# Four PSUM banks for lone up-projections, scores of the next block beside the value product of the last, and a deeper pipeline for the first token blocks

## The chip, the cores and the metric

One core of a Trainium2 chip runs the whole program. The metric is the device time of one launch in microseconds (us), lower is better. TensorE (PE in the profile, with its weight loads as PEld), VectorE (DVE), ScalarE (ACT), GpSimd (POOL) and SyncE (SP, which here only issues DMAs) each work through an instruction list of their own, in the order in which the program was written, and wait for one another through semaphores.

## The reference

Sliding-window causal attention over 8 sequences of 576 tokens with 8 heads of 64, followed by a two-layer network with a quick-GELU on each of the 4608 tokens. The weights are called `moe_`, but there is one expert and no routing.

```python
scores = (1 / sqrt(64)) * matmul(q, k.transpose(0, 1, 3, 2))     # q, k, v: (8, 8, 576, 64)
mask   = (rel >= 0) & (rel < 64)                                  # rel = query position - key position
attn   = softmax(where(mask, scores, -1e9))
x      = matmul(attn, v), heads side by side                      # (4608, 512)
h      = x @ w_in                                                 # (512, 2048)
out    = (h * sigmoid(1.702 * h)) @ w_out                         # (4608, 512), float32
```

## The kernel before

**Tiles.** The 4608 tokens are 36 *blocks* of 128 tokens (number m) and 9 *chunks* of 512 tokens (number ch, four blocks each). A sequence b has 4.5 blocks of its own, so its rows come in five pieces i of 128 tokens, the fifth of 64. A query reaches 64 keys back, so 64 queries need 128 keys.

**Attention for a block.** `cast_qk` turns a piece of q and k to bf16 (`rows_q`, `rows_k`), `cast_v` that of v. The rows are transposed to `qkt`, either by TensorE (`turn_pe`: eight transposes into the PSUM tile `turn`, then one copy by DVE for q, and after it one by ACT for k) or by a transposing DMA (`turn_dma`). `scores(m)` is 16 small matmuls into the PSUM tile `S`; `exp(m)` on ACT gives `E`; `mask(m)` on DVE multiplies with the band and gives `PT`; `pv(m)` is 16 matmuls into `Tacc`, whose spare column holds the row sum; `norm(m)` on DVE is a reciprocal `rc` and a multiplication to `xs`. `xs` is transposed to `xT`, by TensorE (`x_mm` into `pxt`, then the ACT copy `x_out`) or by DMA (`x_dma`).

**The network.** `up(ch, f, nf, t0, nt)` computes a 128x512 piece of h in one PSUM bank (`hps`): 16 matmuls of 128 columns, 8 of 256 or 4 of 512. ACT takes the tanh (`th`, L284), DVE makes `gT` = (tanh + 1) * h (L287). `down(ch, i)` is four matmuls of 512 columns, and every fourth `down` finishes 128 tokens, which `down_out` copies on ACT (`o_sb`) and sends out, with the DMA issued from ACT's queue (L309).

**PSUM.** Eight banks: `psS` 2 (one `S`), `psT` 2 (one `Tacc` or `pxt`), `psH` 2 (two `hps`, or a `turn`), `psO` 2 (two `ops`, or a `turn` or `pxt`).

**Stages.** The order is written out by hand (`manual_schedule`):
1. *First blocks*: m = 0 to 2, with attention alone, since no `xT` is there yet. `warm(n)` puts n matmuls on nothing into TensorE's list.
2. *Lone ups of chunk 0*: 16 `up`, with `pv(3)` between them.
3. *Downs of chunk 0*: 16 `down`, with the transposes of pieces (0,4) and (1,0) and the attention of block 4 between them.
4. *Lone ups of chunk 1*: four rounds (m = 4 to 7) of four `up`, each with the attention of block m+1 and the arrival of a piece.
5. *Slots 32 to 143*: in each slot one `up` of chunk ch, then one `down` of chunk ch-1. The tables `pe` and `post` hang the rest on slots: a function in `pe[s]` comes between the slot's `up` and `down`, one in `post[s]` at the start of the slot. `scores(m)` stand at `slot_s[m]`, and `mask(m)` and `pv(m)` at `slot_s[m] + 2`, `mask` in `post`, `pv` in `pe`. From block 12 on (chunk 3) `xs` goes to `xT` by DMA.
6. *Last downs*: 16 `down` of chunk 8.

From sequence 3 on the pieces are loaded by `load_bf16` from POOL's queue, transposed by `turn_dma`, and `shift_v` on POOL makes the second copy of v.

Of the kernel before, what the change touches and what calls it, by code (L numbers as in the profile page):

```python
# [9 lines left out]
H = 8  # L10
# [18 lines left out]
def kernel(  # L29
# [17 lines left out]
    th_pool = ctx.enter_context(tc.tile_pool(name="th", bufs=2))  # L47
# [221 lines left out]
    H_of, O_of = {}, {}  # L269

    def up(ch, f, nf, t0, nt):

        ps = psH.tile([P, nf, nt], fp32, name="hps", tag="H")
        for g in range(nf):
            for c in range(4):
# [6 lines left out]
                )  # L282
        th = th_pool.tile([P, nf, nt], bf16, name="th", tag="th")
        nc.scalar.activation(out=th[:], in_=ps[:], func=AF.Tanh, scale=0.851)  # L284
        if (ch, f // 4) not in gT:
# [4 lines left out]
        )  # L290

# [14 lines left out]
    def down_out(ch, tsub):  # L306
        o_sb = ob_pool.tile([P, DM], fp32, name="o_sb", tag="o_sb")
        nc.scalar.activation(out=o_sb[:], in_=O_of.pop((ch, tsub))[:], func=AF.Copy, scale=0.5)  # L308
        nc.scalar.dma_start(out=out_tiled[:, ch * 4 + tsub, :], in_=o_sb[:])  # L309
# [7 lines left out]
    DA = (nc.vector, nc.scalar)  # L317

# [9 lines left out]
    for m in range(3):  # L328
        arrive(0, m + 1)
        if m == 1:  # L330
            for j in range(4):
                load_w_in(j)
        mask(m)
        pv(m)
        norm(m)
        turn_pe(psO, "O", 0, m + 1)
        x_mm(m, psO, "O")
        x_out(m)
        scores(m + 1)
        exp(m + 1)  # L340
        if m < 2:
            warm(4)
# [15 lines left out]
    up(0, 4, 4, P, P)  # L358
    up(0, 4, 4, 2 * P, P)
    up(0, 0, 4, 3 * P, P)  # L360
    up(0, 4, 4, 3 * P, P)
    for f in range(8, 16):
        up(0, f, 1, 0, 512)


    for i in range(16):
        if i % 4 == 0 and i > 0:
            down_out(0, i // 4 - 1)
        if i == 10:
# [4 lines left out]
        if i == 11:  # L374
            scores(4)
            exp(4)
        if i == 13:
# [3 lines left out]
            arrive(1, 1)  # L381
        down(0, i)
    x_mm(4, psH, "H")
    x_out(4)
    turn_pe(psH, "H", 1, 1)
# [3 lines left out]
    b2 = iter([lambda i=i: load_f32(2, i) for i in range(5)])  # L389
    next(b2)()  # L390
    for m in range(4, 8):
        scores(m + 1)
        exp(m + 1)
        t0 = (m % 4) * P
        up(1, 0, 4, t0, P)
        up(1, 4, 4, t0, P)
        mask(m + 1)
        pv(m + 1)
        norm(m + 1)
        if m < 7:  # L400
            arrive(1, m - 2)
        next(b2)()
        if m >= 6:
            cast_qk(2, m - 6, (nc.gpsimd, nc.gpsimd))
# [27 lines left out]
    for m in range(9, NM):  # L432
        if m < 12:
            at(slot_pv[m] + 1, lambda m=m: x_mm(m, psT, "T"), [lambda m=m: x_out(m)])
    for m in range(9, NM):
        at(slot_s[m], lambda m=m: scores(m), [lambda m=m: exp(m)])
        later(slot_pv[m], lambda m=m: mask(m))
        at(slot_pv[m], lambda m=m: pv(m), [lambda m=m: norm(m)])
        if m >= 12:
            later(slot_pv[m] + 1, lambda m=m: x_dma(m))  # L440

    for i in range(2, 5):
        at(32 + 2 * (i - 2), lambda i=i: cast_qk(2, i, (nc.gpsimd, nc.gpsimd)))
        at(32 + 2 * (i - 2), lambda i=i: turn_dma(2, i))
        at(32 + 2 * (i - 2), lambda i=i: cast_v(2, i))
# [64 lines left out]
```

## Time and profile before

| what | value |
|---|---|
| time, median of 3 runs | 351.66 us (350.82 to 353.08) |
| the profiled execution: its own time, its span | 355.03 us, 353.3 us |
| TensorE busy | 310.0 us (88%) |
| VectorE, ScalarE, GpSimd busy | 163.4 us (46%), 158.0 us (45%), 133.5 us (38%) |
| mean granted TensorE clock | 0.985 of full |
| HBM traffic | 36.70 MB read, 9.44 MB written |

Times within the execution are counted from the start of the span. A row of a timeline has start, duration, engine, line, operation, `out<-in`, shapes and a count, and in brackets the idle time of the engine before it with what ended that. A row of the waits says which engine and line stood idle, for whom, for how long in all, how often, and the longest. A matmul's duration includes its way through the pipeline, so that consecutive matmuls overlap in the rows; what TensorE's time is spent on is read from start to start.

### The profile page before, as it was taken

The numbers are of one execution on the slowest core, as the hardware profiler recorded it, in microseconds if no ns is written. First come the engines' busy times: TensorE is split into PE (matmuls) and PEld (weight loads), VectorE is DVE, ScalarE is ACT, GpSimd is POOL, SyncE is SP. The second block draws the span as 40 slices with busy tenths as digits, with TensorE's granted clock in tenths as the row PEclk, the third lists the DMA queues.
The fourth block names the chain that finished last, engine by engine and source line by source line (L and its number), as shares of the span: only waits on it lengthen the run. The fifth ranks groups of instructions, "written<-read, shape, count | busy, mean of one in ns | idle before, by whom it ended". The sixth has DMA issues, their size and how long they took to land.

```text
span 353.3 us, 7859 instructions
## 1 busy us (share of the span) xinstructions
PE 310.0 (88%) x3240; PEld 187.1 (53%) x3240; DVE 163.4 (46%) x285; ACT 158.0 (45%) x249; POOL 133.5 (38%) x190
## 2 busy tenths in 40 slices
PE   2777897677789996999999999999999999999995
PEld 1447343466666664676665665665444444444442
DVE  4535531456554453545445545544545544533400
ACT  3463424555444443444454454444445444444421
POOL 3670043745398589234983923492000000000000
PEclk9998999998899999999999999999999999999999
DMA  9999899946499999799999999993343331110021
GB/s 171 187 182 204 153 202 243 237 95 121 84 121 139 148 158 135 80 132 168 148 117 163 185 148 143 126 113 77 87 94 87 79 76 45 46 59 31 32 75 73
DMA packets 164579, 43.83 MB, mean 124 GB/s; under 512 B 155840, under 2 KB 159936, under 8 KB 164544
## 3 DMA queue, kind: packets, MB, share of 16 engines
q0 software_dynamic: 74544, 13.05, 53.5%
q1 hardware_dynamic: 84816, 20.85, 36.0%
q10 hardware_dynamic: 5184, 9.44, 7.4%
q8 instruction: 25, 0.41, 0.5%
q14 instruction: 10, 0.08, 0.1%
HBM read 36.70 MB, written 9.44 MB: 131 GB/s over the span
## 4 chain that ended last, share of the span: by engine, by line
PE 60%; DVE 17%; ACT 12%; DMA 6%; issue 2%; ACTq 1%; SPq 0%
PE ops L298 26%; PE hps L276 26%; DVE gT L287 8%; ACT th L284 7%; DVE PT L209 6%; PE Tacc L223 4%; DMA xT_dma<-xs 4%; PE S L194 3%; DMA stage<-in_k_dram 3%; ACT E L204 2%; DVE xs L236 2%; ACT o_sb L308 1%; ACT qkt L177 1%; PE turn L171 1%; DVE qkt L177 1%
## 5 line engine op out<-in xcount | busy, mean ns | idle before, releaser
L287 DVE SCALAR_TENSOR_TENSOR gT<-th,hps 128x512 bf16<-128x512 bf16 x144 | 98.9, 687 | 142.4 <-ACT th L284 142.0
L284 ACT ACTIVATE th<-hps 128x512 bf16<-128x512 f32 x144 | 85.9, 597 | 143.2 <-PE hps L276 131.1
L298 PE MATMUL ops<-w_out_sb,gT 128*128 128x512 bf16 x576 | 143.8, 380 | 0.0
L276 PEld LDWEIGHTS <-w_in_sb 128*128 128x128 bf16 x1376 | 102.9, 100 | 51.9 <-issue 6.0
L276 PE MATMUL hps<-xT_dma,w_in_sb 128*128 128x128 bf16 (+2 forms) x704 | 99.4, 282 | 3.1 <-DMA xT_dma<-xs 3.1
L298 PEld LDWEIGHTS <-gT 128*128 128x128 bf16 x576 | 51.2, 98 | 51.5
L276 PE MATMUL hps<-xT_pe,w_in_sb 128*128 128x128 bf16 (+1 forms) x672 | 52.9, 235 | 2.4 <-DVE gT L287 2.1
L102 POOL DMA_DIRECT2D v_nat<-in_v_dram x25 | 21.5, 860 | 43.7 <-issue 42.5
L204 ACT ACTIVATE E<-S 128x1024 bf16<-128x1024 f32 x36 | 36.7, 1020 | 2.1 <-PE S L194 1.6
L308 ACT ACTIVATE o_sb<-ops 128x512 f32<-128x512 f32 x36 | 21.5, 598 | 25.5 <-PE ops L298 25.4
L223 PEld LDWEIGHTS <-PT 128*64 128x64 bf16 x576 | 12.6, 114 | 33.5 <-DVE PT L209 33.4
L223 PE MATMUL Tacc<-v_nat,PT 128*64 128x65 bf16 x256 | 14.8, 202 | 12.5 <-DVE PT L209 12.5
L236 DVE TENSOR_TENSOR xs<-Tacc,rc 128x512 bf16<-128x512 f32 x36 | 24.9, 691 | 1.2
L223 PE MATMUL Tacc<-v_off,PT 128*64 128x65 bf16 x320 | 16.6, 201 | 9.6 <-DVE PT L209 9.6
L209 DVE TENSOR_TENSOR PT<-E,mask_None 128x1024 bf16<-128x1024 bf16 x28 | 20.3, 725 | 4.2 <-ACT E L204 4.2
L101 POOL DMA_DIRECT2D rows_k<-in_k_dram x25 | 21.6, 863 | 0.0
L101 POOL DMA_DIRECT2D rows_q<-in_q_dram x25 | 21.4, 856 | 0.0
L86 POOL CAST v_off<-stage 64x512 bf16<-64x512 f32 x15 | 9.1, 610 | 26.7 <-DMA stage<-in_v_dram 26.6
L194 PE MATMUL S<-qkt 64*128 64x64 bf16 x576 | 16.0, 196 | 3.6 <-ACT qkt L177 3.5
L106 POOL COPY v_off<-v_nat 64x528 bf16<-64x528 bf16 x25 | 16.8, 676 | 6.0 <-DMA v_nat<-in_v_dram 5.0
L194 PEld LDWEIGHTS <-qkt 64*128 64x128 bf16 x576 | 11.2, 98 | 12.0 <-issue 5.7
L108 POOL COPY v_off<-v_nat 64x528 bf16<-64x528 bf16 x20 | 13.7, 684 | 1.2
(39 smaller groups left out, 106.8 us busy)
## 6 DMA issues: line engine op xcount, KB each, us to landing
out_dram<-o_sb ACTq DMA_DIRECT2D x36, 256.0 KB, 2.5
stage<-in_q_dram SPq DMA_DIRECT2D x12, 256.0 KB, 5.1
stage<-in_k_dram SPq DMA_DIRECT2D x12, 256.0 KB, 5.1
stage<-in_v_dram SPq DMA_DIRECT2D x12, 256.0 KB, 5.2
rows_q<-in_q_dram POOLq DMA_DIRECT2D x20, 128.0 KB, 5.4
rows_k<-in_k_dram POOLq DMA_DIRECT2D x20, 128.0 KB, 6.0
v_nat<-in_v_dram POOLq DMA_DIRECT2D x20, 128.0 KB, 5.2
w_in_sb<-in_moe_w_in_dram POOLq DMA_DIRECT2D x4, 512.0 KB, 10.5
```

What stands on the lines that cost most here:

```text
L101: nc.gpsimd.dma_start(out=heads(rows[b % 2][w][0:n, i, :]), in_=rows_of(src, b, i))
L102: nc.gpsimd.dma_start(out=v_nat[b % 2][0:n, i, :, 0:D], in_=rows_of(v, b, i))
L194: nc.tensor.matmul(st[:, h % 2, t * 256 + hp * 64 : t * 256 + hp * 64 + 64], lhsT=src[part, 2 * hp + 1, 64 * j : 64 * j + 128], rhs=src[pa ...
L204: nc.scalar.activation(out=E_of[m][:], in_=S_of.pop(m)[:], func=AF.Exp, scale=scale)
L209: nc.vector.tensor_tensor(out=pt[:].rearrange("p a f -> p (a f)"), in0=E_of.pop(m)[:].rearrange("p a f -> p (a f)"), in1=masks[z][:].rearr ...
L223: nc.tensor.matmul(acc[t * 64 : t * 64 + 64, h // 4, (h % 4) * 66 : (h % 4) * 66 + 65], lhsT=pt[:, epos : epos + 64], rhs=win, start=True, ...
L236: nc.vector.tensor_tensor(out=xs[:].rearrange("p (b h d) -> p b h d", b=2, h=4), in0=view[:, :, :, 0:D], in1=rc[:].to_broadcast([P, 2, 4, D]),
L276: nc.tensor.matmul(ps[:, g, :], lhsT=w_in_sb[:, c, (f + g) * P : (f + g + 1) * P], rhs=xT[ch][:, c, t0 : t0 + nt], start=(c == 0), stop=(c ...
L284: nc.scalar.activation(out=th[:], in_=ps[:], func=AF.Tanh, scale=0.851)
L287: nc.vector.scalar_tensor_tensor(out=gT[ch, f // 4][:, f % 4 : f % 4 + nf, t0 : t0 + nt], in0=th[:], scalar=1.0, in1=ps[:], op0=ALU.add, o ...
L298: nc.tensor.matmul(O_of[ch, tsub][:, :], lhsT=gT[ch, j][:, f, tsub * P : (tsub + 1) * P], rhs=w_out_sb[:, 4 * j + f, :], start=(j == 0 and ...
L308: nc.scalar.activation(out=o_sb[:], in_=O_of.pop((ch, tsub))[:], func=AF.Copy, scale=0.5)
```

## The change

- `up` is cut into `up_mm`, `up_th` and `up_g`. With `wide=True` every second `hps` takes a bank of `psO`, so the lone ups turn through four banks. `th_pool` has three buffers for two.
- First blocks: `turn_pe(m + 1)` now stands ahead of `mask(m)`, `pv(m)` and `norm(m)`, and `x_mm(m)`, `x_out(m)` come behind `scores(m + 1)`, `exp(m + 1)`. `warm(2)` stands twice in each block, `warm(6)` ahead of the first `up`. A quarter of `w_in` is loaded a block earlier.
- Downs of chunk 0: pieces (0,4) and (1,0) arrive at i = 9 for 10, `scores(4)` at i = 10 for 11, `x_mm(4)` goes behind `down` 14. The output DMAs of chunks 0 and 1 are issued from SP's queue for ACT's.
- Lone ups of chunk 1: `turn_pe` of the next piece moves to the start of the round, the first `up` stands ahead of `scores`, two `up` stand between `scores(m + 1)` and `pv(m + 1)`, and the casts of q and k (`arrive`) are done by POOL for DVE and ACT.
- Slots: `scores(m + 1)` stand with `pv(m)` in one slot, `mask(m + 1)` two slots later, `pv(m + 1)` at the next place of the table, two to four slots on. Chunk 3's blocks 12 to 15 go through TensorE's transposes for DMA. The loads of the later sequences are spaced three slots apart for one.

```diff
-    th_pool = ctx.enter_context(tc.tile_pool(name="th", bufs=2))
+    th_pool = ctx.enter_context(tc.tile_pool(name="th", bufs=3))
...
-            how = "pe" if ch < 3 else "dma"
+            how = "pe" if ch < 4 else "dma"
...
+    def up_mm(ch, f, nf, t0, nt, wide=False):
+
+        pool, tag = (psO, "O") if wide and next(turns) % 2 else (psH, "H")
+        ps = pool.tile([P, nf, nt], fp32, name="hps", tag=tag)
...
-        nc.scalar.dma_start(out=out_tiled[:, ch * 4 + tsub, :], in_=o_sb[:])
+        eng = nc.sync if ch < 2 else nc.scalar
+        eng.dma_start(out=out_tiled[:, ch * 4 + tsub, :], in_=o_sb[:])
...
     for m in range(3):
         arrive(0, m + 1)
-        if m == 1:
-            for j in range(4):
+        if m == 0:
+            load_w_in(0)
+        elif m == 1:
+            for j in range(1, 4):
                 load_w_in(j)
+        turn_pe(psO, "O", 0, m + 1)
         mask(m)
         pv(m)
         norm(m)
-        turn_pe(psO, "O", 0, m + 1)
+        warm(2)
+        scores(m + 1)
+        exp(m + 1)
+        warm(2)
         x_mm(m, psO, "O")
         x_out(m)
-        scores(m + 1)
-        exp(m + 1)
-        if m < 2:
-            warm(4)
...
-    up(0, 0, 4, 0, P)
-    up(0, 0, 4, P, P)
+    warm(6)
     mask(3)
+    up(0, 0, 4, 0, P, wide=True)
     pv(3)
     norm(3)
-    up(0, 0, 4, 2 * P, P)
-    up(0, 4, 4, 0, P)
-    x_mm(3, psO, "O")
+    up(0, 0, 4, P, P, wide=True)
+    up(0, 0, 4, 2 * P, P, wide=True)
+    x_mm(3, psT, "T")
...
-        if i == 10:
+        if i == 9:
             arrive(0, 4)
             arrive(1, 0)
...
-            arrive(1, 1)
+            arrive(1, 1, GG)
         down(0, i)
-    x_mm(4, psH, "H")
-    x_out(4)
-    turn_pe(psH, "H", 1, 1)
+        if i == 14:
+            x_mm(4, psT, "T")
+            x_out(4)
     down_out(0, 3)
...
     for m in range(4, 8):
+        t0 = (m % 4) * P
+        turn_pe(psT, "T", 1, m - 3)
+        u = up_mm(1, 0, 4, t0, P, wide=True)
         scores(m + 1)
+        u = up_th(*u)
         exp(m + 1)
-        t0 = (m % 4) * P
-        up(1, 0, 4, t0, P)
-        up(1, 4, 4, t0, P)
+        up_g(*u)
+        u = [up_mm(1, f, 4, t0, P, wide=True) for f in (4, 8)]
+        u = [up_th(*x) for x in u]
         mask(m + 1)
         pv(m + 1)
+        up_g(*u[0])
         norm(m + 1)
+        up_g(*u[1])
         if m < 7:
-            arrive(1, m - 2)
-        next(b2)()
+            arrive(1, m - 2, GG)
+        load_f32(2, m - 4)
...
-        up(1, 8, 4, t0, P)
-        x_mm(m + 1, psO, "O")
+        up(1, 12, 4, t0, P, wide=True)
+        x_mm(m + 1, psT, "T")
         x_out(m + 1)
-        if m < 7:
-            turn_pe(psO, "O", 1, m - 2)
-        up(1, 12, 4, t0, P)
...
-    slot_s = {9: 32, 10: 36, 11: 40, 12: 43, 13: 46}
-    for m in range(14, NM):
-        slot_s[m] = max(slot_s[m - 1] + 3, 4 * (m - 4) - 2)
-    slot_pv = {m: s + 2 for m, s in slot_s.items()}
...
+    slot_pv = {8: 32, 9: 34, 10: 38, 11: 42, 12: 45}
+    for m in range(13, NM):
+        slot_pv[m] = max(slot_pv[m - 1] + 3, 4 * (m - 4) - 2)
+    for m in range(8, NM):
+        s = slot_pv[m]
+        if m + 1 < NM:
+            at(s, lambda m=m: scores(m + 1), [lambda m=m: exp(m + 1)])
+            later(s + 2, lambda m=m: mask(m + 1))
+        if m > 8:
+            at(s, lambda m=m: pv(m), [lambda m=m: norm(m)])
+            if m < 16:
+                at(s + 1, lambda m=m: x_mm(m, psT, "T"), [lambda m=m: x_out(m)])
+            else:
+                later(s + 2, lambda m=m: x_dma(m))
...
-            use = slot_s[(S * b + P * i) // P]
-            at(max(free, 38) + i, lambda b=b, i=i: load_bf16(b, i))
-            at(use - 5, lambda b=b, i=i: turn_dma(b, i))
-            at(use - 5, lambda b=b, i=i: shift_v(b, i))
+            use = slot_pv[(S * b + P * i) // P - 1]
+            come = max(free, 36) + 3 * i
+            at(come, lambda b=b, i=i: load_bf16(b, i))
+            at(max(use - 5, come + 4), lambda b=b, i=i: turn_dma(b, i))
+            at(max(use - 5, come + 4), lambda b=b, i=i: shift_v(b, i))
```

Three places show what this makes of the engines' lists. (Most of the changed kernel's line numbers are higher, by 1 at the start and by up to 14 further down.) The first is ACT in the first blocks, one block's instructions; before:

```order
L95 CAST rows_k_100<-stage_94 128x512
L177 COPY qkt_103<-turn 128x4x128
L262 COPY xT_pe<-pxt 128x4x128
L204 ACTIVATE E<-S 128x1024
L95 CAST rows_k_100<-stage_95 128x512
```

And in the changed kernel, where the cast of the next piece of k now stands behind the copy to `xT`, which itself has moved behind the exponential:

```order
L96 CAST rows_k_100<-stage_94 128x512
L178 COPY qkt_103<-turn 128x4x128
L205 ACTIVATE E<-S 128x1024
L263 COPY xT_pe<-pxt 128x4x128
L96 CAST rows_k_100<-stage_95 128x512
```

The same blocks on DVE, before:

```order
L95 CAST rows_q_99<-stage_94 128x512
L209 TENSOR_TENSOR PT<-E,mask_140 128x1024
L234 RECIPROCAL rc<-Tacc 128x8
L236 TENSOR_TENSOR xs<-Tacc,rc 128x512
L177 COPY qkt_103<-turn 128x4x128
```

In the changed kernel the copy of the transposed q of the next piece has moved from behind `xs` to ahead of the mask:

```order
L96 CAST rows_q_99<-stage_94 128x512
L178 COPY qkt_103<-turn 128x4x128
L210 TENSOR_TENSOR PT<-E,mask_140 128x1024
L235 RECIPROCAL rc<-Tacc 128x8
L237 TENSOR_TENSOR xs<-Tacc,rc 128x512
```

The last place is DVE in the slots, from the mask of one block to the mask of the next, three slots on. Before, one `gT` stands between the mask and the reciprocal, which waits for that block's `pv`:

```order
L209 TENSOR_TENSOR PT<-E,mask_None 128x1024
L287 SCALAR_TENSOR_TENSOR gT<-th,hps 128x4x128
L234 RECIPROCAL rc<-Tacc 128x8
L236 TENSOR_TENSOR xs<-Tacc,rc 128x512
L287 SCALAR_TENSOR_TENSOR gT<-th,hps 128x4x128 x2
L209 TENSOR_TENSOR PT<-E,mask_None 128x1024
```

In the changed kernel two stand there, and one behind `xs`, so the mask is an instruction of a slot earlier against its `pv`:

```order
L210 TENSOR_TENSOR PT<-E,mask_None 128x1024
L296 SCALAR_TENSOR_TENSOR gT<-th,hps 128x4x128 x2
L235 RECIPROCAL rc<-Tacc 128x8
L237 TENSOR_TENSOR xs<-Tacc,rc 128x512
L296 SCALAR_TENSOR_TENSOR gT<-th,hps 128x4x128
L210 TENSOR_TENSOR PT<-E,mask_None 128x1024
```

More of the change, by code (lines that the diff above doesn't have):

```diff
@@ L1 @@
+import itertools
 from contextlib import ExitStack
@@ L268 @@
     gT = {}
-    H_of, O_of = {}, {}
-    def up(ch, f, nf, t0, nt):
-        ps = psH.tile([P, nf, nt], fp32, name="hps", tag="H")
+    O_of = {}
+    turns = itertools.count()
+    def up_mm(ch, f, nf, t0, nt, wide=False):
+        pool, tag = (psO, "O") if wide and next(turns) % 2 else (psH, "H")
+        ps = pool.tile([P, nf, nt], fp32, name="hps", tag=tag)
         for g in range(nf):
@@ L425, in later @@
         post.setdefault(slot, []).append(g)
-    slot_s = {9: 32, 10: 36, 11: 40, 12: 43, 13: 46}
-    for m in range(14, NM):
-        slot_s[m] = max(slot_s[m - 1] + 3, 4 * (m - 4) - 2)
-    slot_pv = {m: s + 2 for m, s in slot_s.items()}
[L432 to L440, printed above, removed]
+    slot_pv = {8: 32, 9: 34, 10: 38, 11: 42, 12: 45}
[12 more added lines that the diff above has]
+                later(s + 2, lambda m=m: x_dma(m))
+    at(32, lambda: load_f32(2, 4))
     for i in range(2, 5):
-        at(32 + 2 * (i - 2), lambda i=i: cast_qk(2, i, (nc.gpsimd, nc.gpsimd)))
-        at(32 + 2 * (i - 2), lambda i=i: turn_dma(2, i))
-        at(32 + 2 * (i - 2), lambda i=i: cast_v(2, i))
+        at(4 * i + 24, lambda i=i: cast_qk(2, i, GG))
+        at(4 * i + 24, lambda i=i: turn_dma(2, i))
+        at(4 * i + 24, lambda i=i: cast_v(2, i))
     for b in range(3, B):
```

24 lines of the change are left out of this document (15 added, 9 removed).

## The prediction

> **What bounds the kernel now.** I read the stages first. In the windows below the columns are the window, its length, busy time of PE, PEld, DVE, ACT and POOL with counts, the granted clock, the DMA share and GB/s; the cuts are the first `up`, the first `down`, the first `up` of chunk 1, that of slot 32, and the last downs.
>
> ```profile
> 0.00:24.13 24.13, 13.23 (x164) 7.80 (x165) 11.22 (x30) 10.20 (x15) 15.03 (x29) 1.00 1.08 177
> 24.13:46.19 22.06, 17.97 (x186) 12.58 (x181) 11.28 (x18) 10.46 (x18) 1.73 (x4) 0.92 1.07 186
> 46.19:66.57 20.38, 17.40 (x141) 8.50 (x140) 4.94 (x11) 7.52 (x13) 9.30 (x16) 1.00 1.09 224
> 66.57:100.38 33.81, 24.50 (x414) 21.21 (x408) 19.18 (x33) 17.55 (x31) 18.19 (x28) 0.90 0.64 115
> 100.38:334.68 234.30, 222.03 (x2280) 130.45 (x2281) 116.05 (x193) 108.69 (x169) 89.27 (x116) 1.00 1.06 110
> ```
>
> TensorE is the bound, but only from slot 32 on is it nearly full (222.03 of 234.30 us). In the two stages of lone ups it stands for 4.1 of 22.06 and 9.3 of 33.81 us, with DVE and ACT half idle too: a chain, not an engine. Then I asked what TensorE waits for, stage by stage from the second on (two rows each for the lone ups of chunk 0 and the downs of chunk 0, one for the lone ups of chunk 1, two for the slots):
>
> ```profile
> PE hps L276 <- DVE gT L287: 2.1, 5, 0.4
> PE Tacc L223 <- DVE PT L209: 2.0, 1, 2.0
> ...
> PE turn L171 <- ACT rows_k L95: 2.0, 1, 2.0
> PE S L194 <- ACT qkt L177: 0.9, 1, 0.9
> ...
> PE Tacc L223 <- DVE PT L209: 8.7, 4, 2.3
> ...
> PE Tacc L223 <- DVE PT L209: 9.0, 26, 0.8
> PE hps L276 <- DMA xT_dma<-xs: 3.1, 2, 2.7
> ```
>
> Nearly all of it is `pv` waiting for the mask: once for 2.0 us, four times for 8.7, 26 times for 9.0.
>
> **Slots: mask, banks and `xT`.** PE at two places of the late slots:
>
> ```profile
> 247.14 1.03 PE L276 MATMUL hps<-xT_dma,w_in_sb 128*128 128x512 bf16 x4
> 248.10 0.41 PE L194 MATMUL S<-qkt 64*128 64x64 bf16 x16
> 248.44 1.04 PE L298 MATMUL ops<-w_out_sb,gT 128*128 128x512 bf16 x4
> ...
> 251.04 1.03 PE L276 MATMUL hps<-xT_dma,w_in_sb 128*128 128x512 bf16 x4
> ...
> 252.35 0.22 PE L223 MATMUL Tacc<-v_off,PT 128*64 128x65 bf16 x1 [0.28 <-DVE PT L209]
> ...
> 252.73 1.04 PE L298 MATMUL ops<-w_out_sb,gT 128*128 128x512 bf16 x4
> ```
>
> Four wide matmuls take 0.86 us (four at 0.216; the 1.03 holds the way through the pipeline). From 247.14 to 248.44 is 1.30: the scores cost 0.44, of which 0.10 is the switch from `up` and 0.34 the matmuls. From 251.04 to 252.73 is 1.69: `pv` costs 0.83, of which 0.38 is work and 0.45 the wait for a mask that stands two slots behind its scores, plus a switch. In the changed table the mask is issued one or two slots ahead of `pv`, so 9.0 us go. What is late next: `pv` needs the `Tacc` bank, which `x_out` of the block before frees two slots earlier, so nothing. `scores` and `pv` side by side may save one switch of 0.10 in 26 blocks: 0 to 2.6 us; I take 1, as no row shows the two adjacent. Blocks 12 to 15 no longer wait for their DMA (3.1 us, of which 0.4 belongs to chunk 4 and stays in place: 2.7 go), but take a transpose each:
>
> ```profile
> 108.15 0.39 PE L257 MATMUL pxt<-ident,xs 128*128 128x128 bf16 x4
> 108.37 1.03 PE L298 MATMUL ops<-w_out_sb,gT 128*128 128x512 bf16 x4
> ...
> 109.47 1.05 PE L276 MATMUL hps<-xT_pe,w_in_sb 128*128 128x128 bf16 x16
> ```
>
> That is 0.22 for the transposes and 0.24 by which the `down` behind them (1.10) exceeds 0.86: 4 x 0.46 = 1.8 us. The four ACT copies lie beside TensorE's work (ACT is busy 108.69 of 234.30). Sum of the slots: -9.0 - 1.0 - 2.7 + 1.8 = **-10.9** (bounds -14 and -4).
>
> **First blocks and lone ups of chunk 0.** Rows of one block's cycle, of several engines, in order of time:
>
> ```profile
> 6.03 0.61 PE L171 MATMUL turn<-ident,rows_k 128*128 128x128 bf16 x4 [0.79 <-ACT rows_k L95]
> ...
> 6.67 0.42 DVE L177 COPY qkt<-turn 128x512 bf16<-128x512 bf16 x1 [2.10 <-PE turn L171]
> ...
> 9.35 0.61 ACT L95 CAST rows_k<-stage 128x512 bf16<-128x512 f32 x1
> 9.48 0.69 DVE L209 TENSOR_TENSOR PT<-E,mask 128x1024 bf16<-128x1024 bf16 x1 [1.25 <-ACT E L204]
> ...
> 10.23 0.26 PE L223 MATMUL Tacc<-v_off,PT 128*64 128x65 bf16 x1 [1.85 <-DVE PT L209]
> ...
> 10.81 0.61 PE L171 MATMUL turn<-ident,rows_q 128*128 128x128 bf16 x4
> ...
> 12.83 0.59 ACT L262 COPY xT_pe<-pxt 128x512 bf16<-128x512 bf16 x1
> 12.99 0.61 PE L194 MATMUL S<-qkt 64*128 64x64 bf16 x16 [0.44 <-ACT qkt L177]
> 13.53 1.89 PE L315 MATMUL idle<-mask_None,ident 128*128 128x512 bf16 x4
> ...
> 14.56 0.61 ACT L95 CAST rows_k<-stage 128x512 bf16<-128x512 f32 x1
> ```
>
> Here a wide matmul takes 0.43 us (four in 1.89 less the pipeline's 0.17), twice that of the slots: TensorE runs at half rate. A block takes 5.21 us now (cast of k 9.35 to 14.56). In the changed lists a longer ring closes, since DVE has the q copy ahead of the mask and ACT the `xT` copy ahead of the next cast of k: cast 0.66, k transposes 0.64, q copy 0.42, mask 0.75, `pv` 0.58, `warm(2)` 0.86, scores 0.54, `warm(2)` 0.86, transposes of `xs` 0.66, copy to `xT` 0.59 (each with its hand-over). That is 6.56 us, **1.35 longer**. From the cast at 9.35: next ones at 15.9 and 22.5, scores(3) done at 26.9, `warm(2)` and `x_mm(2)` to 28.2, `warm(6)` 1.3 us at full rate or 2.6 at half: first `up` at 29.5 to 30.8 for 24.13. I take 30.0.
>
> The clock decides in this range. Two windows around the one wait of 2.0 us:
>
> ```profile
> 25.10:28.50 3.40, 1.39 (x35) 1.18 (x33) 1.97 (x3) 1.33 (x3) 0.00 (x0) 1.00 1.24 207
> 28.50:31.90 3.40, 3.40 (x40) 3.40 (x37) 1.59 (x3) 0.75 (x2) 0.00 (x0) 0.56 1.24 208
> ```
>
> After 3.4 us in which TensorE was busy 1.39 (41%), the next 3.4 had a granted clock of 0.56. The changed first blocks hold pauses of that kind, so I count them at half rate throughout. The Trainium skill, page "TensorE: Matmul & The Clock Gate", section "Why this matters for your kernels", asks only that gaps stay below about 3 us; by that no pause here would slow TensorE once it is up, and the first `up` would come some 2 us earlier, an estimate. The row speaks against it: a gap of 2.0 us was enough.
>
> Now the lone ups, before:
>
> ```profile
> 37.05 2.02 PE L276 MATMUL hps<-xT_pe,w_in_sb 128*128 128x512 bf16 x8 [0.41 <-DVE gT L287]
> ...
> 39.48 2.01 PE L276 MATMUL hps<-xT_pe,w_in_sb 128*128 128x512 bf16 x8 [0.41 <-DVE gT L287]
> ```
>
> Two ups in 2.43 us, because the third needs the bank that `gT` of the first frees. With four banks TensorE's 0.87 each (0.89 in pieces of 128) is the bound, as ACT needs 0.60 and DVE 0.69. 16 ups 14.1, `pv(3)` 0.38, `x_mm(3)` 0.25, one wait for `xs` behind `gT` 0.4: 15.1 for 22.06. First `down` at 45.1 for 46.19: **-1.1** (bounds -3 and +5). What the four banks gain, the first blocks give back.
>
> **Downs of chunk 0.** ACT at the wait of 2.0 us:
>
> ```profile
> 53.30 0.60 ACT L308 ACTIVATE o_sb<-ops 128x512 f32<-128x512 f32 x1 [2.85 <-PE ops L298]
> 56.16 0.34 ACTq L309 DMA_DIRECT2D out_dram<-o_sb  x1
> 56.54 0.62 ACT L95 CAST rows_k<-stage 64x512 bf16<-64x512 f32 x1 [2.64 <-DMA stage<-in_k_dram]
> ```
>
> ACT's list stood at the output DMA from 53.90 to 56.16, and the cast of k behind it. With that DMA on SP's queue the wait goes; SP has only loads for chunk 2 behind it, which are not needed before slot 32. The bill: 16 downs 13.8, transposes of three pieces 1.4, scores 0.44, `pv` 0.48, `x_mm` 0.46, and two new waits, as the pieces now come in the middle of the downs (0.3 for k, 0.6 for the copies): 17.5 for 20.38, **-2.9** (bounds -3.5 and -1).
>
> **Lone ups of chunk 1.** Now 33.81 us, 8.45 a round. In the changed order the ring of a round is: transposes to the first copy 0.73, q copy and k copy 1.06, tanh of the first `up` 0.58, exponential 1.02, mask 0.75, hand-over and a `gT` ahead of the reciprocal 0.72, `rc` and `xs` 0.93, `x_mm` 0.48, `xT` copy 0.64: 6.9 us. TensorE's work in it is 4 x 0.89 and about 1.4, so 5.0, with no wait above 0.9 and 72% busy, far from the 41% that cost the clock. Four rounds, from the first `up` to that of slot 32, 27.1: **-6.7** (bounds -9 and -2, the latter if the casts on POOL come late or slow DVE's masks).
>
> **Sum.** -1.1 - 2.9 - 6.7 - 10.9 = -21.6 on the profiled execution's 355.03 (353.3 of span and 1.7 around it): 333.4. The runs shown have a median of 351.66, 3.4 lower; I put the same difference on it: **330.0 us**.
>
> **Rivals.**
> (a) *First blocks*: w_in's first quarter is now loaded beside the pieces of q, k and v, with the DMAs already full in the first row of windows (1.08). If the cast of piece 3 waits 3 us and `warm(6)` runs at half rate, the first `down` comes at 49.8: +4.7, **334.7**. For it: the ring has no slack. Against: the casts now come later anyway.
> (b) *The mask wait becomes another wait*, for `Tacc` or for `xs`: the 9.0 and 1.0 stay, **340.0**. Against: DVE is busy half of the slots' time.
> (c) *Rounds stay at 8.45 us*, held by casts on POOL: 6.7 stay, **336.7**.
> (d) *The change doesn't do what it says*: ups stay at 1.22 us a piece, with the chain of tanh and `gT` in place of the bank. In chunk 0 16 x 0.35 = 5.6: **335.6**. Against: 0.60 and 0.69 us are below 0.87.
> (e) *Slower than before*: the loads of sequences 3 to 7 stand 4 or 5 slots ahead of their transposes, for 3 to 20 before. The row for pieces of k, from issue to landing:
>
> ```profile
> DMA to landing us min/median/max: 2.3/5.4/11.4
> ```
>
> A slot takes 234.30 / 112 = 2.1 us, so five are 10.5, and the transpose has another 10.5 to the scores. From a landing of about 16 us on, each of 23 blocks would be late; at 1.1 us each that is 25 us, and the kernel 1% slower, **355.2**. Against it: 5.4 is a third of that, and spacing relieves the queue.
>
> **How the numbers follow.** Forecast 0.50, (a) 0.18, (b) 0.12, (c) 0.09, (d) 0.05, (e) 0.06. The range takes in the four partial cases, and two of them at once at the upper end: 343; at the lower end all bounds but that of the first blocks: 323. A change under 1% (about what a measurement of this kernel can tell) needs three of (a) to (d) together: 0.03. Faster by over 1%: 0.91, slower by over 1%: 0.06.
>
> **What would show it.** The wait of `pv` for `PT` in the slots below 2 us for 9.0; the first `up` near 30 and the first `down` near 45; no ACT queue time at output DMAs before slot 32; rounds of 6.9 us with a clock of 1.00; slot 32 near 90. I am wrong if TensorE waits for the ring of the first blocks beyond 31 us, if `pv` still waits, or if a transposing DMA turns up as releaser of scores.

## The result and the profile after

The changed kernel takes 326.85 us in the median of four runs (325.9 to 327.95), the kernel before, run in turn with it, 352.37 (350.82 to 356.11): a ratio of 0.929, with a 95% interval of 0.923 to 0.935. 330.0 was forecast, in a range of 323 to 343. A second run of the same kernel on another chip (below) gave 326.49 and a ratio of 0.928. The profiled execution took 327.95 us, the longest of the four, 326.2 of them span.

The stages of the changed kernel, cut as before at the first `up`, the first `down`, the first `up` of chunk 1, that of slot 32 and the last downs (same columns as in the prediction):

```profile
0.00:30.60 30.60, 17.25 (x171) 9.55 (x175) 11.53 (x31) 11.67 (x16) 14.97 (x29) 1.00 1.13 193
30.60:45.52 14.92, 14.87 (x181) 10.84 (x180) 10.38 (x17) 9.45 (x16) 1.40 (x3) 1.00 1.09 194
45.52:62.40 16.88, 16.51 (x123) 8.13 (x124) 4.72 (x9) 6.23 (x11) 13.73 (x22) 1.00 0.98 197
62.40:87.85 25.45, 22.18 (x428) 19.25 (x426) 17.92 (x32) 17.22 (x29) 15.52 (x23) 1.00 0.85 172
87.85:307.70 219.85, 214.13 (x2265) 133.07 (x2298) 115.98 (x193) 110.76 (x173) 90.42 (x122) 1.00 1.15 116
```

Stage by stage against before: 30.60 for 24.13 us, 14.92 for 22.06, 16.88 for 20.38, 25.45 for 33.81, and 219.5 for 234.3 from the first `up` of slot 32 to the `down` behind the last `up` (at 307.35 and 334.68; the last row above ends 0.35 later). The first blocks lose 6.5 us; the lone ups and downs of chunk 0 gain 7.1 and 3.5, the lone ups of chunk 1 8.4, the slots 14.8. TensorE is now nearly full in every stage but the first and the rounds of chunk 1.

What TensorE waits for in the slots, with sum, number of times and longest in us:

```profile
PE ops L310 <- issue: 4.3, 27, 0.2
PE S L195 <- DMA qkt<-rows_k: 0.7, 1, 0.7
PE hps L279 <- ACT xT_pe L263: 0.7, 1, 0.7
```

The 9.0 us for `PT` and the 3.1 for `xT` are gone. The first row is no wait of the chip: the records show three matmuls in the `down` behind each `pv` where the kernel issues four, and the missing one looks like a pause of 0.16. A block of the late slots on TensorE:

```profile
231.10 1.03 PE L279 MATMUL hps<-xT_dma,w_in_sb 128*128 128x512 bf16 x4
232.06 0.41 PE L195 MATMUL S<-qkt 64*128 64x64 bf16 x16
232.39 0.22 PE L224 MATMUL Tacc<-v_off,PT 128*64 128x65 bf16 x1
...
233.00 0.81 PE L310 MATMUL ops<-w_out_sb,gT 128*128 128x512 bf16 x3 [0.16 <-issue]
233.65 1.03 PE L279 MATMUL hps<-xT_dma,w_in_sb 128*128 128x512 bf16 x4
```

From 231.10 to 233.65 are 2.55 us; less 1.73 for the eight wide matmuls of an `up` and a `down` leaves 0.82 for scores and `pv`, where they cost 0.44 and 0.83 before. The `pv` follows 0.33 behind the scores, so there is no switch between the two.

### The profile page after: what moved, and what is told of

Read it like the earlier page. It is cut to its first block, busy times and chain, and to the rows that moved or that the text cites. A ratio compares the mean times of both kernels' runs of the same rounds, so it can differ in the third digit from the quotient of the medians.

```text
span 326.2 us, 7851 instructions
## 1 busy us (share of the span) xinstructions
PE 299.4 (92%) x3226; PEld 187.2 (57%) x3266; DVE 161.2 (49%) x281; ACT 158.8 (49%) x249; POOL 136.0 (42%) x198
## 4 chain that ended last, share of the span: by engine, by line
PE 83%; ACT 6%; DVE 4%; DMA 3%; issue 2%; SPq 0%; ACTq 0%
PE ops L310 36%; PE hps L279 35%; PE Tacc L224 4%; PE S L195 4%; PE idle L328 2%; DMA qkt<-rows_k 2%; PE turn L172 2%; ACT th L290 2%; DVE PT L210 1%; ACT xT_pe L263 1%; DMA stage<-in_k_dram 1%; ACT E L205 1%; DVE qkt L178 1%; PE pxt L258 1%; ACT rows_k L96 1%
## 5 line engine op out<-in xcount | busy, mean ns | idle before, releaser
L310 PE MATMUL ops<-w_out_sb,gT 128*128 128x512 bf16 x542 | 136.7, 379 | 4.8 <-issue 4.5
L279 PEld LDWEIGHTS <-w_in_sb 128*128 128x128 bf16 x1376 | 99.9, 98 | 45.8 <-issue 2.4
L310 PEld LDWEIGHTS <-gT 128*128 128x128 bf16 x576 | 52.9, 98 | 52.1
L279 PE MATMUL hps<-xT_dma,w_in_sb 128*128 128x256 bf16 (+1 forms) x446 | 82.2, 318 | 0.1
L279 PE MATMUL hps<-xT_pe,w_in_sb 128*128 128x128 bf16 (+1 forms) x927 | 64.6, 224 | 1.0 <-ACT xT_pe L263 0.7
L107 POOL COPY v_off<-v_nat 64x528 bf16<-64x528 bf16 x25 | 15.6, 625 | 10.2 <-DMA v_nat<-in_v_dram 9.5
L224 PE MATMUL Tacc<-v_nat,PT 128*64 128x65 bf16 x256 | 14.8, 202 | 0.2 <-DVE PT L210 0.2
L178 DVE COPY qkt<-turn 128x512 bf16<-128x512 bf16 (+1 forms) x10 | 4.0, 398 | 20.6 <-PE turn L172 20.6
```

The source lines that it names most:

```text
L224: nc.tensor.matmul(acc[t * 64 : t * 64 + 64, h // 4, (h % 4) * 66 : (h % 4) * 66 + 65], lhsT=pt[:, epos : epos + 64], rhs=win, start=True, ...
L279: nc.tensor.matmul(ps[:, g, :], lhsT=w_in_sb[:, c, (f + g) * P : (f + g + 1) * P], rhs=xT[ch][:, c, t0 : t0 + nt], start=(c == 0), stop=(c ...
L310: nc.tensor.matmul(O_of[ch, tsub][:, :], lhsT=gT[ch, j][:, f, tsub * P : (tsub + 1) * P], rhs=w_out_sb[:, 4 * j + f, :], start=(j == 0 and ...
```

## The experiments

Eleven kernels beside the changed one, each with a kernel before on its chip. Stage times below are from their profiled executions.

### The first blocks: order, warming matmuls, ring

**The order of before in the first blocks**, with its `warm(4)` and with the first quarter of `w_in` loaded where it was, the rest as changed:

```diff
     for m in range(3):
         arrive(0, m + 1)
...
-        turn_pe(psO, "O", 0, m + 1)
         mask(m)
         pv(m)
         norm(m)
-        warm(2)
-        scores(m + 1)
-        exp(m + 1)
-        warm(2)
+        turn_pe(psO, "O", 0, m + 1)
         x_mm(m, psO, "O")
         x_out(m)
+        scores(m + 1)
+        exp(m + 1)
+        if m < 2:
+            warm(4)
...
-    warm(6)
```

> The changed kernel with the first blocks of before (transposes of the next piece behind norm, xT copy ahead of scores, warm(4), no warm(6)) and all else as changed. Theory: the new order of the first blocks is a longer ring and costs time; the first up comes near 24 us instead of 30.6, the first down near 40 instead of 45.5, and the whole kernel takes about 321.5 us, 5 to 6 less than the changed kernel's 326.9. Rival 1: the weights and the pieces of q, k and v are what the stage waits for, so the time comes back as DMA waits in the ups or in the downs of chunk 0, and the total stays within 1.5 us of 326.9. Rival 2: without warm(6) the ups run at half the clock for a window and lose 2 us of the gain: about 323.5.

Measured: 323.23 us, ratio 0.912 (0.905 to 0.919); first `up` at 24.12, first `down` at 39.87. Both places are as the theory had them. The time is 1.7 above its 321.5 and at rival 2's 323.5, but not for the rival's reason: from first `up` to first `down` it takes 15.75 us, 0.83 longer than the changed kernel and not 2. To the first `down` the stages gain 5.65 us, the medians only 3.6, as the changed kernel's stages are those of its longest execution.

**The changed order without its `warm` calls:**

```diff
-        warm(2)
         scores(m + 1)
         exp(m + 1)
-        warm(2)
...
-    warm(6)
```

> The changed kernel without its twelve warming matmuls (two warm(2) in each of three blocks, warm(6)), order otherwise as changed. Theory: the first warm(2) of a block stands in the ring ahead of the scores and the second ahead of the transposes of xs, 0.86 us each at half rate, so the ring falls from 6.5 to about 4.8 us; first up near 23.5 for 30.6; the ups then begin at half rate, which costs at most 1.7 us in one window of 3.4 us; total about 321.5 us, 5 less than 326.9. Rival: the warming is what keeps the ups at full rate; without it they run at half rate for several windows, and the total is 327 or more.

Measured: 322.93 us, ratio 0.911 (0.904 to 0.918); first `up` at 24.20, first `down` at 39.77. The ring was to fall to 4.8 us and the time to 321.5; the casts of k show 5.21 and 5.24 a block, where the old order has 5.21 and 5.53. So the new order by itself costs nothing against the old one (with its `warm(4)`), and gains nothing. The warming matmuls are the whole loss: 3.9 us by the medians, 5.4 by the spans of the profiled executions. They stand in the ring, and they buy little: without them the 15.57 us from first `up` to first `down` are 0.65 longer than with them.

```profile
0.00:24.20 24.20, 10.37 (x156) 7.28 (x157) 10.79 (x30) 10.84 (x15) 12.28 (x26) 1.00 1.14 194
24.20:39.77 15.57, 15.52 (x181) 11.50 (x181) 11.07 (x18) 10.23 (x18) 2.95 (x5) 1.00 1.09 181
```

**A shorter ring:** no warming, the casts of a block directly behind the exponential of the block two before it, the mask between the transposes and their copies (`turn_pe` here takes functions to put there).

```diff
-        arrive(0, m + 1)
+        if m == 0:
+            cast_qk(0, 1, DA)
+        cast_v(0, m + 1)
...
-        turn_pe(psO, "O", 0, m + 1)
-        mask(m)
+        turn_pe(psO, "O", 0, m + 1, (lambda: mask(m),))
...
         exp(m + 1)
-        warm(2)
+        if m < 2:
+            cast_qk(0, m + 2, DA)
         x_mm(m, psO, "O")
```

> The changed kernel without its warming matmuls, and with the first blocks' chain shortened: the casts of block m+2 stand right behind the exponential of block m, and the mask of block m stands between the turn of block m+1 and its copies. Theory (the first up is set by the ring of casts, turn, copies, scores and exponential alone): the ring falls from 5.2 us without warming to about 4.0 us per block, the first up comes at 20 to 21 us, and the kernel ends at 319 to 320 us. Rival (loads set the end there: weights and the rows of the next blocks come no earlier): TensorE waits for transfers where the ring was short, and the time stays at 322 to 323 us, that of the kernel without warming.

Measured: 319.90 us, ratio 0.909 (0.903 to 0.916), beside 326.49 for the changed kernel on the same chip. The casts of k on ACT show the ring:

```profile
9.29 0.62 ACT L96 CAST rows_k<-stage 128x512 bf16<-128x512 f32 x1
13.29 0.61 ACT L96 CAST rows_k<-stage 128x512 bf16<-128x512 f32 x1
17.33 0.61 ACT L96 CAST rows_k<-stage 128x512 bf16<-128x512 f32 x1
```

4.02 us a block, first `up` at 20.68, as the theory had it. The first `up` comes 8.4 us earlier than in the changed kernel of that chip (29.05), the kernel ends 6.6 us earlier. 1.35 us are given back in the lone ups of chunk 0 (16.27 for 14.92), whose first matmuls run at half rate.

**Single warming matmuls in the pauses of that ring**, where nothing waits for them:

```diff
         for w in range(2):
+            for g in mid if w else ():
+                g()
             for hp in range(4):
...
-        turn_pe(psO, "O", 0, m + 1, (lambda: mask(m),))
+        turn_pe(psO, "O", 0, m + 1, (lambda: mask(m),), (lambda: warm(1),))
         pv(m)
+        warm(1)
...
         x_mm(m, psO, "O")
+        if m < 2:
+            warm(1)
```

> The kernel with the shorter ring of the first blocks, with one warming matmul each in three of TensorE's pauses per block (between the transposes of q and k, behind the value product, behind the transposes of xs). Theory (TensorE runs at half rate in the first blocks because it stands still too much): at some 85% busy it reaches full rate inside the first blocks, the transposes, scores and value products on the ring halve, the ring falls from 4.04 to about 3.4 us, the first ups run at full rate from the start, and the time falls by 2 to 3 us, to 317 us. Rival (the pauses are too short, and the rate does not rise): a half-rate warming matmul of 0.43 us in each pause pushes the ring's work back by 0.2 to 0.4 us a block, and the time is that of the shorter ring or up to 1.5 us more, 320 to 321.5 us.

Measured: 319.41 us, ratio 0.905 (0.899 to 0.912): the fastest version here, but not to be told from the ring without warming. TensorE reached full rate inside the first blocks, as the theory had it, but only in the last of them: the casts of k stand at 9.32, 13.29 and 17.32 us, a ring of 4.0 us still and not 3.4, and the sum of 317 us was missed. An early warming matmul, a later one, and the first `up`:

```profile
8.69 0.63 PE L332 MATMUL idle<-mask_None,ident 128*128 128x512 bf16 x1
...
16.46 0.38 PE L332 MATMUL idle<-mask_None,ident 128*128 128x512 bf16 x1
...
20.09 1.06 PE L283 MATMUL hps<-xT_pe,w_in_sb 128*128 128x128 bf16 x16
```

From 16.2 us on TensorE is at full rate, after it had worked without a pause since 11.72, and the first `down` comes at 36.04 for 36.95. But chunk 1 starts at 53.84 in the one kernel and 53.83 in the other: the downs of chunk 0 now last 17.80 for 16.88. On POOL and SP:

```profile
36.18 0.18 POOL L369 CAST stage<-w_out_sb 1x1 f32<-1x1 bf16 x1 [10.34 <-DMA w_out_sb<-in_moe_w_out_dram]
...
36.38 0.73 SPq L82 DMA_DIRECT2D stage<-in_q_dram  x1
```

The loads of pieces (0,4) and (1,0) are held back, by that one-element copy, until w_out has landed, at 36.2 us here and at 35.8 with the ring alone. TensorE then waits 0.75 us for the cast of k, and that cast 0.75 for its load. The first blocks are no longer the only bound at this point. Whether earlier loads would free the 0.9 us was not tried.

### The banks of the lone ups

**`up` with two banks again:** `wide=True` left out at every call.

> The changed kernel with every up in the two banks of psH (wide off), all else as changed. Theory: an up in chunk 0 goes back from 0.87 to 1.22 us, 16 x 0.35 = 5.6 us later to the first down; in the rounds of chunk 1 the fourth up waits for a bank by 0.2 to 0.5 us, and that lies in the ring or not: 0 to 2 us; total 332.5 to 334.5. Rival: the rate of the lone ups comes from tanh and gT, not from the bank: total unchanged at 327.

Measured: 333.08 us, ratio 0.939 (0.932 to 0.947), within the expectation. TensorE's waits in the lone ups of chunk 0, and one of them:

```profile
PE hps L279 <- DVE gT L296: 2.6, 7, 0.4
...
43.29 2.02 PE L279 MATMUL hps<-xT_pe,w_in_sb 128*128 128x512 bf16 x8 [0.41 <-DVE gT L296]
45.72 2.02 PE L279 MATMUL hps<-xT_pe,w_in_sb 128*128 128x512 bf16 x8 [0.41 <-DVE gT L296]
```

Two ups per 2.43 us are back, and the stage is 19.4 us instead of 14.92: 4.5 us, for the 5.6 expected. The rounds of chunk 1 take 26.96 us (65.88 to 92.84) for 25.45. Together the four banks are worth about 6 us.

**The casts of chunk 1's pieces on VectorE and ScalarE again:** `arrive(1, ...)` without `GG`.

> The changed kernel, but the casts of chunk 1's pieces are made by VectorE and ScalarE again, not by GpSimd. Theory (the round of the lone ups of chunk 1 is a ring of ScalarE and VectorE work, as the forecast had it): a cast of q on VectorE and of k on ScalarE, 0.6 us each, stand in a ring of 6.5 us; a round becomes 7.1 us or more, the stretch of lone ups 2 to 3 us longer, and the kernel 328.5 to 329.5 us. Rival (TensorE's own work is the bound in the rounds): the stretch keeps its 25.5 us and the kernel stays within 1 us of the changed one.

Measured: 328.48 us, ratio 0.931 (0.925 to 0.936); the first `up` was at 30.88 here. The rounds of chunk 1:

```profile
62.67:88.90 26.23, 22.28 (x429) 19.32 (x426) 19.12 (x35) 18.72 (x32) 16.15 (x24) 1.00 0.82 169
```

26.23 us from the first `up` of chunk 1 to that of slot 32, for 25.45 in the changed kernel; the other kernels whose rounds are unchanged lie between 25.42 and 26.16. So the 2 to 3 us of the theory are not there, and what the casts do to the rounds is not clear of that spread. The rival's "within 1 us" was missed by the medians (1.6 more) and kept by the spans (0.9 more).

### The downs of chunk 0

**Outputs of chunks 0 and 1 from ScalarE's queue again:**

```diff
-        eng = nc.sync if ch < 2 else nc.scalar
-        eng.dma_start(out=out_tiled[:, ch * 4 + tsub, :], in_=o_sb[:])
+        nc.scalar.dma_start(out=out_tiled[:, ch * 4 + tsub, :], in_=o_sb[:])
```

> The changed kernel, but the four output transfers of chunk 0 (and those of chunk 1) are issued by ScalarE again, as before the change. Theory (the 3.5 us that the downs of chunk 0 lost came from ScalarE standing still behind its output issues): the stretch from the first down to chunk 1's first up grows from 16.9 to 19.5 to 20.4 us and the kernel by about 2.5 to 3.5 us, to 329.5 to 330.5 us. Rival (it came from the order of the blocks' work in that stretch): 16.9 us stays, and the kernel within 1 us of the changed one.

Measured: 330.69 us, ratio 0.940 (0.933 to 0.947). The size fits, the place does not. From first `down` to chunk 1 it took 17.40 us for 16.88, with TensorE waiting 0.63 for the cast of k: 0.5 of the 3.5 us that the stage gained. Another 1.6 us are a later first `up` (30.67 for 29.05), which this edit doesn't touch (the last section has its reason). The rest is at an output of chunk 1, in the slots; two rows of ACT and then one of TensorE:

```profile
97.67 0.60 ACT L320 ACTIVATE o_sb<-ops 128x512 f32<-128x512 f32 x1
101.58 0.34 ACTq L321 DMA_DIRECT2D out_dram<-o_sb  x1
...
103.39 1.05 PE L279 MATMUL hps<-xT_pe,w_in_sb 128*128 128x128 bf16 x16 [2.02 <-DVE gT L296]
```

ACT stood still from 98.27 to 101.58 at that issue, the next tanh came late, and TensorE waited 2.02 us for `gT`. So an output issue on ACT can hold the chain up, but what it held up was in the slots. What the issue stood for is in the trace: ACT first waits there for the semaphore of an earlier transfer, here of the transposing DMA of q that went out at 94.43 and landed at 101.51. In the kernel before, the issue at 56.16 waited in the same way for a load of k, of a later piece than the cast behind it needs:

```profile
50.25 0.97 SPq L81 DMA_DIRECT2D stage<-in_k_dram  x1
```

It landed at 56.08. The load of that cast's own k had gone out at 40.33 and landed at 43.78. With the issue back on ACT in the changed kernel, the transfers that the issues at 49.87 and 53.32 wait for had landed by then, and neither stood still for one.

### The slots

**The slot table of before** (scores two slots ahead of `pv`, mask in `pv`'s slot, loads as in that table), with chunk 3's `xT` still from TensorE:

```diff
-            at(s, lambda m=m: scores(m + 1), [lambda m=m: exp(m + 1)])
-            later(s + 2, lambda m=m: mask(m + 1))
...
-            at(s, lambda m=m: pv(m), [lambda m=m: norm(m)])
+        at(slot_s[m], lambda m=m: scores(m), [lambda m=m: exp(m)])
+        later(slot_pv[m], lambda m=m: mask(m))
+        at(slot_pv[m], lambda m=m: pv(m), [lambda m=m: norm(m)])
```

> The changed kernel with the slot table of before: scores alone in a slot, mask and pv two slots later; xT of chunk 3 still by TensorE, loads spaced as changed. Theory: each of 26 blocks again takes 0.45 us more (0.35 wait for the mask and 0.10 for a second switch of TensorE), more in chunk 2 where the wait was up to 0.8: 12 to 15 us, total 339 to 342, with the wait of pv for PT back at about 9 us. Rival: the gain of the slots came from the spaced loads and from the transposes of chunk 3, and the table is worth less than 4 us: total under 331.

Measured: 340.25 us, ratio 0.960 (0.950 to 0.969): 13.4 us more than the changed kernel, and in the slots the wait is back:

```profile
PE Tacc L224 <- DVE PT L210: 8.6, 27, 0.8
```

**The changed kernel again**, as the measure for its chip:

> The changed kernel again, as the measure for the three runs beside it on this chip. Both theories: 326 to 328 us, a ratio of 0.925 to 0.93 against before.

Measured: 326.49 us, ratio 0.928 (0.922 to 0.934).

**Masks early, but scores one slot ahead of `pv`:**

```diff
-            at(s, lambda m=m: scores(m + 1), [lambda m=m: exp(m + 1)])
+            at(max(s - 1, 32), lambda m=m: scores(m + 1), [lambda m=m: exp(m + 1)])
```

> The changed kernel, but scores(m+1) are issued one slot ahead of the value product of block m, with the masks where the change has them. Theory (the two small matmul groups, put side by side, save one change of shape each, 0.10 us in 26 slots): 2.6 us longer than the changed kernel, about 329.5 us, with the four-slot period late in the kernel 0.1 longer per block and no new waits of TensorE. Rival (only the earlier masks paid in the slots): the same as the changed kernel within 0.7 us.

Measured: 334.09 us, ratio 0.948 (0.942 to 0.955), 7.6 us more than the changed kernel. The pair's price is as the theory had it:

```profile
228.36 0.41 PE L195 MATMUL S<-qkt 64*128 64x64 bf16 x16
228.70 1.04 PE L310 MATMUL ops<-w_out_sb,gT 128*128 128x512 bf16 x4
229.57 1.03 PE L279 MATMUL hps<-xT_dma,w_in_sb 128*128 128x512 bf16 x4
230.53 0.22 PE L224 MATMUL Tacc<-v_off,PT 128*64 128x65 bf16 x1
```

The `pv` group now pays a switch of its own (0.96 from the start of an `up` of 0.86), and there is no wait for the mask. From the scores of one late block to the next it takes 7.83 to 7.84 us for 7.73: 0.105 in each. The other 5 us the theory did not have: the scores of block 13 came a slot too early for their keys,

```profile
PE S L195 <- DMA qkt<-rows_k: 3.1, 1, 3.1
```

and from these scores to the next it takes 4.6 us longer than in the changed kernel; what the wait leaves of that is TensorE at half rate behind it (a granted clock of 0.50 from 117.17 to 120.58, where a `down` of 0.86 takes 1.68).

**Scores beside `pv`, but the mask in `pv`'s own slot:**

```diff
-            later(s + 2, lambda m=m: mask(m + 1))
+            later(slot_pv[m + 1], lambda m=m: mask(m + 1))
```

> The changed kernel, but each mask stands at the head of the value product's own slot, as before the change, not one or two slots ahead of it; the scores of the next block still stand between the slot's up and the value product. Theory (the earlier place of the mask is what took the 9 us of waiting): the wait comes back whole, 0.35 us in each of some 26 blocks, and the kernel is 9 us longer than the changed one, 335.5 us. Rival (the scores of 0.34 us that now run ahead of the value product cover a mask that is late by 0.35): the wait of the value product stays below 1 us in all, and the kernel within 1 us of the changed one, 326 to 327.5 us.

Measured: 328.98 us, ratio 0.932 (0.925 to 0.939), the span 326.4 for 326.2. The wait for the mask is 0.5 us over all slots; the nine did not come back. DVE and then TensorE in one late block:

```profile
231.47 0.69 DVE L210 TENSOR_TENSOR PT<-E,mask_None 128x1024 bf16<-128x1024 bf16 x1
...
231.86 0.41 PE L195 MATMUL S<-qkt 64*128 64x64 bf16 x16
232.21 0.22 PE L224 MATMUL Tacc<-v_off,PT 128*64 128x65 bf16 x1
```

The mask ends at 232.16, and `pv` starts at 232.21, 0.35 behind the scores for 0.33 in the changed kernel: the scores cover a late mask to within 0.02 us. In the changed kernel the mask of such a block ends 3.5 us ahead (228.90 for 232.39). The time is 2.1 us above the changed kernel's by the medians, 1.1 by the ratio and by the slots alone, so the rival's "within 1 us" is not quite reached. Together with the run before: either half of the change is enough to remove the wait.

**Chunk 3's `xT` by transposing DMAs again:**

```diff
-            how = "pe" if ch < 4 else "dma"
+            how = "pe" if ch < 3 else "dma"
...
-            if m < 16:
+            if m < 12:
```

> The changed kernel, but chunk 3's xT comes by transposing DMAs as before the change, not by TensorE. Theory (the forecast's two terms stand: 2.7 us of waiting for those DMAs against 1.8 us for four transposes): about 0.9 us longer than the changed kernel, 327.4 us, with TensorE waiting for the DMA of xT again. Rival (with the masks one or two slots earlier xs is ready earlier too, and the DMA lands in time): no wait, the 1.8 us come off, 324.7 us.

Measured: 331.93 us, ratio 0.940 (0.935 to 0.946): 4 to 5 us more by ratio and medians, 6.0 in the slots of the profiled execution (by the output copies that frame them), neither the 0.9 of the theory nor the -1.8 of the rival. One wait returns, and four windows around it show what it costs (PE busy and, third from the right, the granted clock):

```profile
PE hps L279 <- DMA xT_dma<-xs: 3.2, 1, 3.2
...
117.80:121.20 3.40, 3.40 (x40) 2.30 (x37) 1.38 (x3) 1.19 (x2) 2.95 (x5) 1.00 1.62 236
121.20:124.47 3.27, 0.11 (x2) 0.01 (x1) 0.60 (x1) 0.60 (x1) 3.19 (x4) 0.88 2.08 118
124.47:127.80 3.33, 3.01 (x48) 2.71 (x50) 0.78 (x2) 1.41 (x2) 2.29 (x4) 0.50 1.84 203
127.80:131.20 3.40, 3.39 (x22) 2.31 (x22) 0.71 (x2) 0.50 (x2) 2.74 (x4) 0.60 2.01 168
```

A wait of 3.2 us, and behind it a clock of 0.50 and then 0.60 for 6.7 us, in which 1.7 and 1.4 us of work are lost again: 6.3 us, less the 1.8 for the four transposes that go, is 4.5; the other 1.5 were not traced. The Trainium skill, page "TensorE: Matmul & The Clock Gate", section "Why this matters for your kernels", warns of gaps above about 3 us; this one agrees. Of the two gaps of 2.0 us in the kernel before, the one in the lone ups (1.39 us busy in a window of 3.4) cost the clock as well, the one between the downs did not (1.00 over that stage). Neither did the 2.7 us that the kernel before waited for the same DMA: its clock is 1.00 over all slots. The last section shows what separates them.

## Why the prediction was right

The sum of -21.6 came out as -27.1 between the two profiled executions (355.03 to 327.95), and as -25.5 between the medians. Some of the closeness of the total is luck: the forecast took 3.4 us off because the profiled execution of before lay that far above the median, and the changed one lies only 1.1 above. The stages together were 5.5 too small, the total 3.15. Two readings of the working are off without changing it: the wait for the mask is 19.7 of the 27.8 us of waits listed, not nearly all, and the bounds named for the lower end give 324, not 323.

- **First blocks and lone ups of chunk 0**: right. Ring 6.5 us for 6.56 (casts of k at 9.37, 15.88 and 22.35), first `up` at 30.60 for 30.0, first `down` at 45.52 for 45.1. Half rate throughout was right for this execution: behind the ring's last transposes a warming matmul still has 0.63 us, for 0.38 at full rate. It was not so in every one (last section). What the prediction had only in one clause, that the first blocks give back what the banks gain, is the largest thing left: the warming matmuls cost 3.9 to 5.4 us, and the shorter ring brought chunk 1 forward by another 2.8 (56.65 to 53.83).
- **Downs of chunk 0**: 3.5 for 2.9, but the cause was only partly the one named. ACT's list did stand at the output issue, as the row said, but the issue itself waited for a load of k of a later piece (issued at 50.25, landed at 56.08), the one that the row names. Putting the issue back on ACT brought only 0.5 of the 3.5 back, since in the changed kernel no such transfer was under way at these issues. Two other things changed in that stretch: w_out landed at 36.8 for 39.35, so the pieces' loads went out 2.5 us earlier, and the casts stand elsewhere. What each of these is worth was not told apart.
- **Lone ups of chunk 1**: 8.4 for 6.7. The ring of 6.9 us was an overestimate: rounds take 6.5, and TensorE waits only 0.7 in each, for the copy to `xT`. It is TensorE's own work of 5.8, not the 5.0 that was put down, and that copy which fill the round; the cast experiment agrees. Two banks for four cost 0.8 to 1.5 there; the new order of the round was not taken back by itself, so its share is argued.
- **Slots**: 14.8 for 10.9, the largest miss. *Adjacency* was put at 1.0 and is 0.105 a block in the late slots, 2.7 if all 26 have it: the upper end of the bound. *The mask's* 9.0 us went. The earlier mask that was named as the reason is enough for it, but was not needed: the scores beside `pv` cover a late mask as well, which the prediction didn't see. From the fifth to the 32nd output copy on ACT, which frame the slots, it takes 226.31 us before, 211.63 changed and 223.81 with the old table: the table is worth 12.2 for 10.0 forecast, which is 26 blocks at 0.46 (8.19 to 7.73 in the late ones), 0.35 of it the wait. The rows' 9.0 understated it. *`xT`* was put at -2.7 + 1.8 = -0.9; by the same frame it brought the remaining 2.5, together with the spacing of the loads, which was not tried alone. Taking it back in the changed table cost 4 to 6, since there the wait has a half clock behind it; in the kernel before it had none, so the sum was not wrong to count the wait alone.
- **Rivals**: none of them took place; (d), the banks without use, is refuted by the 6.2 us that two banks cost, (e) by a single wait of 0.7 us of scores for a transposing DMA. That wait was one of the prediction's own signs of being wrong; it came once, and cost next to nothing.

## What to carry to other kernels

A small wait of one engine can be removed by putting work that it must do anyway ahead of the waiting instruction, which also saves a change of shape; here that does the same as moving the other engine's work earlier. Warming matmuls belong in pauses that nothing waits behind: on the ring they cost 4 to 5 us here, beside it nothing. A wait of 2 to 3 us of TensorE can have a half-rate stretch behind it that costs up to as much again; here waits of 2.0, 3.1 and 3.2 us had one, others of 2.0 and 2.7 had none. A DMA issue in the list of a compute engine can make that engine wait for an earlier transfer that it has no use for.

## What was not expected of the hardware

- The granted clock in the windows reads 1.00 over the first 15 us of every kernel here, while a wide matmul takes 0.43 us there and 0.216 later: up to the first change of the clock on record the column tells nothing. For the start the rate has to be read from durations.
- Full rate came after about 4.5 us of TensorE's work without a pause (11.72 to 16.2 in the ring with single warming matmuls). The Trainium skill, page "TensorE: Matmul & The Clock Gate", section "Why this matters for your kernels", asks for at least 4 us of it; the trace agrees. It came behind work with pauses as well, as the next rows show.
- The clock changes in steps of 3.4 us, and what it does goes by how much of the last step TensorE was busy, not by the longest gap. The first blocks of the changed kernel in its second run, from step to step (PE busy, and third from the right the clock):

```profile
11.80:15.16 3.36, 2.77 (x38) 1.59 (x39) 1.41 (x4) 0.93 (x1) 2.82 (x4) 1.00 1.35 217
15.17:18.57 3.40, 1.31 (x29) 0.93 (x28) 1.02 (x2) 1.77 (x4) 2.79 (x4) 1.00 1.19 193
18.58:21.98 3.40, 3.11 (x29) 1.58 (x28) 1.23 (x3) 1.48 (x2) 2.29 (x4) 0.50 1.27 221
21.99:25.39 3.40, 1.59 (x38) 0.95 (x38) 1.67 (x4) 1.22 (x3) 2.66 (x4) 1.00 1.23 203
25.40:28.80 3.40, 3.18 (x19) 1.46 (x12) 0.94 (x2) 1.61 (x2) 0.00 (x0) 0.50 1.24 207
```

  The transposes of q take 0.61 us at 8.28 and 0.39 at 15.28, so the clock rose between the first two rows. Counting the steps from the changes on record, in the traces of all fourteen profiled executions it falls eleven times while the kernel runs, each time behind a step with at most 1.67 us of work, and rises 25 times, each time behind one with 2.77 or more (one of 2.88 passed without a rise). So a gap counts by where it falls. The wait of 2.7 us in the slots of before left 1.68 us of work in its emptiest step, and the clock stayed:

```profile
134.72:138.13 3.41, 1.68 (x19) 0.95 (x16) 1.73 (x2) 1.36 (x3) 3.18 (x5) 1.00 2.46 126
```

- Runs of the same first-block code put the first `up` between 29.05 and 30.94 us (nine profiled executions). The steps fall at other times in each, and with them the pauses of the ring in one step or another: in the five at 29.05 to 29.58 the clock was up for one or two steps inside the first blocks, in the four at 30.60 to 30.94 it rose for the first time at 30.4 us or later.
- The idle time in a row understates a wait: ahead of `pv` the row of before has 0.28, while 0.35 went, since the modelled end of the matmul ahead holds 0.17 of its way through the pipeline.
